# Layer norm's reciprocal root on ScalarE and VectorE, weight padding on GpSimd, and other writers in the tail of an attention and FFN kernel

## The chip, the cores and the metric

The kernel runs on one core of a Trainium2 chip. The metric is device time in microseconds (us) of one execution; the lower it is, the better. The engines are called by their names or by the short forms of the profile: TensorE (PE; PEld is its weight load), VectorE (DVE), ScalarE (ACT), GpSimd (POOL) and SyncE (SP), which issues the DMAs.

## What is computed

The input x (2048 tokens of 512) is normalised, and attention and a gated feed-forward network (FFN) both read the normalised x. There are 32 heads of 16 columns; the FFN is 1792 wide. All tensors are bfloat16.

```python
xn  = (x - mean(x)) / sqrt(var(x) + 1e-5)
q, k, v = split(xn @ wqkv)                 # 32 heads of 16
p   = softmax(q @ k.T / 4)                 # 2048 x 2048 per head
att = (p @ v) @ wo
ffn = (silu(xn @ w1) * (xn @ w3)) @ w2
out = x + att + ffn
```

## The kernel before

**The work.** Tokens stand in 16 tiles of 128. Queries are taken in four chunks of 512, heads in 8 groups of four, because a head's 16 columns, padded to 32, fill one of TensorE's four row groups. A chunk and a head group make 32 jobs; these are cut into 73 units of 128 or 256 queries (the first job in 128, 128, 256, the last four in 128 each).

Each unit goes through two phases. In phase 1 (`p1`) the scores of 128 queries and 512 keys are computed for two heads (L1041) and VectorE takes the row maximum over both at once (L1081, 128x1024 out of PSUM). 1021 such steps make up phase 1; in three of the units one row of heads takes another way, in which ScalarE helps with a `Relu` (`SPLIT`, L1150, L1070). When a unit's maxima are complete, they are negated, split in two bfloat16 numbers (`Z`, L1165, L1167, on GpSimd) and put beside the queries, by DMA transpose, or for the first two and the last four units by TensorE and a ScalarE write (`tile_QT2`, tiles called AQ, L810). Phase 2 (`p2`) can only then start for that unit: TensorE computes the transposed scores with the maximum already subtracted (L1303), and ScalarE takes the exponential of a half-tile of 128x512 (L1316), or of two in neighbouring banks at once (`exp_pair`, L1346), into slots called PT. There are 2048 half-tiles. Then `tile_PV` multiplies by V (L566); a ScalarE write to `U` (L1412), a small DMA round and GpSimd's reciprocal (L1437) and product (L1457) normalise it. The last three units skip that round: VectorE takes a reciprocal (L1402) and a product (L1404) straight from PSUM.

The FFN (`ffn_pair`) has 56 pairs of tiles, each with two ScalarE writes (L856, L860), a tanh (L850) and three GpSimd steps; the pace at which they may start is set by `FFN_LO` and `FFN_HI`, in phase 1 steps. Its results lie in 24 slots `hT`, which the output tiles free. Outputs of the first twelve token tiles are made in one PSUM tile (`tile_OUT`, L921), those of the last four in two parts: `tile_OUTA`, written by ScalarE (L938), and `tile_OUTB`, added by VectorE (L952) and stored.

**The head.** x comes in four DMAs of four tiles. Layer norm goes in eight groups of two tiles (`ln_chunk`): statistics (`STATS`: groups 0 to 3 on VectorE, L599 and L602; groups 4 to 7 on ScalarE, L589 for the mean and L593 for the squares), then in `coef` GpSimd adds epsilon (L613) and raises to the power -1/2 (L616), then in `norm` the tile is normalised (`NORM`: groups 0 to 2 on VectorE, L629; groups 3 to 7 on GpSimd, L639, for which two more small GpSimd steps first form the bias -mean times the reciprocal root, L620 and L622). TensorE transposes the tile (`tile_tr`, L664), ScalarE writes it to `xnT` (L671). Four tiles make a key block of the first head group (`tile_KT`, L695), the first tile also the first queries (`tile_QT`, L792). Their weights are padded to 32 columns by two ScalarE copies (L532, L534). Keys and queries of the other groups (`tile_heads`, L750, then a DMA through memory) and V (`tile_V`, L765) follow.

**The order of the work.** The program is not written in the order in which it runs. A planner at the end of `_build` keeps queues of items for each engine (`expq`, `miscq` and `lazyq` for ScalarE, `redq` and `dveq` for VectorE, a dictionary of queues `poolq` for GpSimd, `spq` for SyncE), each item with a cost written in the code, and at each turn emits the item that could start first (`pick_act`, `pick_dve`, `pick_pool`, `pick_sp`). For TensorE, `pick_pe` weighs the next phase 1 step, the next phase 2 scores, the next piece of an open tile (`col_cand`) and a filler matmul that keeps the array busy (`fill_cand`; into the tokens, ident against xnT). The result is a fixed order for each engine; at run time the engines only wait for each other's semaphores. Scores of phase 1 use PSUM banks 0 to 3, tiles and phase 2 share banks 4 to 7, and after the last maximum all eight. `assign` gives banks to tiles; `ROW_LEAD` and `TOL` say how much ahead of need scores are issued, `PAIR_WAIT` how long an exponential may be held for a pair, `RECENT_MIN` how many columns TensorE should have worked in the last 2.9 us of the plan.

## Time and profile before

| | us |
|---|---|
| median of 3 runs (1196.06 to 1197.04) | 1196.95 |
| the profiled execution | 1196.41 |
| its span (first to last instruction) | 1194.7 |
| VectorE busy | 1172.0 |
| ScalarE busy | 1169.5 |
| TensorE busy | 1154.4 |
| GpSimd busy | 455.3 |

The profile is of one execution. A row of the timeline gives start and duration of a run of like instructions, the engine, the line, the operation, what it writes and reads, the shapes and the count; in square brackets is the idle time of the engine before it, and what ended it. Durations overlap the next instruction of the same engine a little, so the distance from start to start is the step that counts. "Releasers" are inferred from semaphores. A group's row gives busy time, then the mean of one in ns, then the idle time in front of it. TensorE's busy time includes fillers.

### The profile page before, as it was taken

What the parts mean: (1) busy time and instruction counts of PE and PEld (TensorE: products, weight loads), DVE (VectorE), ACT (ScalarE), POOL (GpSimd) and SP (SyncE); (2) the same over time, 40 slices, a digit from 0 to 9 for tenths busy, and PEclk for the clock granted to TensorE, in tenths of its full rate; (3) what the DMA queues carried; (4) which work ended last, traced back from release to release, by engine and by line L of the source; (5) the groups of instructions that cost most, each with busy time, mean ns of one, the idle gap of its engine ahead of it and who ended that gap; (6) DMA issues with size and microseconds to landing.
All of it is one profiled execution on the core that took longest, in us unless ns stands there. A gap on an engine that the chain in (4) does not pass through costs nothing.

```text
span 1194.7 us, 33930 instructions
## 1 busy us (share of the span) xinstructions
PE 1154.4 (97%) x14172; PEld 482.5 (40%) x14172; DVE 1172.0 (98%) x1067; ACT 1169.5 (98%) x2236; POOL 455.3 (38%) x912
## 2 busy tenths in 40 slices
PE   9999999999999999999999999999999999999998
PEld 4433333333334333333334434343333333345554
DVE  8999999999999999999999999999999999999994
ACT  7899999999999999999999999999999999999997
POOL 4453752433432255343422236634222215333320
PEclk9999999999999999999999999999999999999999
DMA  6523222111111021111100122211000111000000
GB/s 183 128 59 83 68 65 79 39 33 41 38 24 36 25 71 40 41 32 31 33 20 24 35 59 51 51 31 37 22 20 20 32 33 43 19 22 18 18 18 25
DMA packets 131189, 52.17 MB, mean 44 GB/s; under 512 B 100068, under 2 KB 131036, under 8 KB 131036
## 3 DMA queue, kind: packets, MB, share of 16 engines
q1 hardware_dynamic: 131036, 50.01, 16.9%
q8 instruction: 111, 1.82, 0.7%
q14 instruction: 42, 0.34, 0.1%
HBM read 38.73 MB, written 6.74 MB: 38 GB/s over the span
## 4 chain that ended last, share of the span: by engine, by line
PE 45%; ACT 44%; DVE 6%; issue 2%; DMA 2%; POOL 1%; ACTq 0%; POOLq 0%
ACT PT L1316 30%; PE ps L562 17%; PE ps L1303 13%; PE ps L566 8%; ACT PT L1346 7%; PE ps L1041 7%; DVE part L1081 6%; ACT zg L856 2%; ACT th L850 1%; ACT ub L860 1%; DMA R<-rd 1%; ACT U L1412 1%; ACT kq L750 1%; PE ps L1663 1%; DMA Lc<-U 0%
## 5 line engine op out<-in xcount | busy, mean ns | idle before, releaser
L1081 DVE TENSOR_REDUCE part<-ps 128x2 f32<-128x1024 f32 x1018 | 1153.0, 1217 | 1.9 <-PE ps L1041 1.7
L1316 ACT ACTIVATE PT<-ps 128x512 bf16<-128x512 f32 x1680 | 889.2, 628 | 5.6 <-PE ps L1303 2.5
L1303 PE MATMUL ps<-QT,KT 32*128 32x256 bf16 (+1 forms) x4672 | 544.5, 259 | 4.7 <-ACT PT L1346 3.7
L1041 PE MATMUL ps<-KT,QT 32*128 32x512 bf16 x2042 | 424.3, 384 | 2.4 <-DVE part L1081 2.3
L1303 PEld LDWEIGHTS ps<-QT,KT 32*128 32x128 bf16 x4672 | 207.4, 92 | 214.1 <-issue 110.7
L1437 POOL TENSOR_TENSOR Rc<-Lc,mone 128x8 f32<-128x8 f32 (+1 forms) x70 | 105.9, 1513 | 294.6 <-DMA Lc<-U 294.4
L1346 ACT ACTIVATE PT<-ps 128x1024 bf16<-128x1024 f32 x184 | 194.6, 1075 | 0.0
L562 PE MATMUL ps<-xnT,ident 128*128 128x512 bf16 (+3 forms) x646 | 177.4, 341 | 17.5 <-DVE part L1081 6.7
L566 PE MATMUL ps<-PT,Vaug 128*17 128x256 bf16 (+1 forms) x4672 | 179.6, 261 | 3.1 <-ACT PT L1316 1.3
L562 PE MATMUL ps<-xnT,w 128*128 128x512 bf16 (+3 forms) x637 | 153.2, 321 | 4.7 <-ACT ub L860 1.3
L1041 PEld LDWEIGHTS ps<-KT,QT 32*128 32x128 bf16 x2042 | 107.8, 91 | 122.5 <-DVE part L1081 56.8
L566 PEld LDWEIGHTS ps<-PT,Vaug 128*17 128x17 bf16 x4672 | 84.2, 89 | 89.1 <-issue 69.5
L562 PEld LDWEIGHTS ps<-xnT,ident 128*128 128x128 bf16 x646 | 47.4, 97 | 99.9 <-ACT PT L1316 44.5
L562 PEld LDWEIGHTS ps<-xnT,w 128*128 128x128 bf16 x637 | 44.9, 97 | 85.6 <-issue 52.9
L562 PE MATMUL ps<-w,hT 128*128 128x512 bf16 (+3 forms) x330 | 75.1, 315 | 0.0
L837 POOL TENSOR_TENSOR a<-zg,ub 128x512 f32<-128x512 bf16 x56 | 64.5, 1152 | 21.6 <-ACT ub L860 21.6
L839 POOL TENSOR_TENSOR hT<-a,t 128x512 bf16<-128x512 f32 x56 | 71.0, 1267 | 2.4
L1188 POOL TENSOR_TENSOR mx<-part 128x16 f32<-128x16 f32 (+1 forms) x67 | 14.1, 210 | 141.0 <-DVE part L1081 140.5
L1457 POOL TENSOR_TENSOR wk_on<-U,R 128x256 bf16<-128x256 f32 (+1 forms) x37 | 23.3, 630 | 85.8 <-DMA R<-rd 85.6
L835 POOL TENSOR_SCALAR t<-th 128x512 f32<-128x512 bf16 x56 | 34.7, 619 | 44.8 <-ACT th L850 43.2
L1457 POOL TENSOR_TENSOR on_b<-U,R 128x256 bf16<-128x256 f32 (+1 forms) x33 | 23.4, 709 | 70.9 <-DMA R<-rd 70.9
L850 ACT ACTIVATE th<-zg 128x512 bf16<-128x512 bf16 x56 | 37.7, 673 | 0.0
(104 smaller groups left out, 574.5 us busy)
## 6 DMA issues: line engine op xcount, KB each, us to landing
w<-in_B_w_dram SPq DMA_DIRECT2D x112, 128.0 KB
R<-rd SPq DMA_DIRECT2D x55, 128.0 KB
QT<-qd SPq DMA_DIRECT2D x31, 128.0 KB
KT<-kd SPq DMA_DIRECT2D x28, 128.0 KB
PT<-in_A_x_dram SPq DMA_DIRECT2D x4, 512.0 KB
xr<-in_A_x_dram SPq DMA_DIRECT2D x16, 128.0 KB
out_dram<-osb SPq DMA_DIRECT2D x16, 128.0 KB
qd<-kq SPq DMA_DIRECT2D x15, 128.0 KB
```

The lines of the kernel that those rows point to most:

```text
L562: return e.matmul(bank(bk)[:, c0 + a:c0 + b], make_lhsT(0, 128), rhs_ap(0)[:, a:b], start=start, stop=stop, **kw)
L566: ins = e.matmul(bank(bk)[32 * i:32 * i + m, c0 + a:c0 + b], make_lhsT(i), rhs if (a, b) == (0, ncols) else rhs[:, a:b], start=start, stop ...
L837: q.append(_Item(lambda e: e.tensor_tensor(a32[:, :], zg[:, ss, :], ub[:, ss, :], ALU.mult), [("zg", ss), ("ub", ss)], [("a32",)], 1.1, 1.25))
L839: q.append(_Item(lambda e: e.tensor_tensor(hT[:, hslot(idx), :], a32[:, :], t1[:, :], ALU.mult), [("a32",), ("t1",)], [("hT", hslot(idx))] ...
L850: lazyq.append(_Item(lambda e: e.activation(th[:, ss, :], zg[:, ss, :], ACTF.Tanh), [("zg", ss)], [("th", ss)], 0.52, cb=part_done))
L1041: ins = e.matmul(bank(2 * sl + i), QT[32 * j:32 * j + 32, qs, q * 128:(q + 1) * 128], KT[32 * j:32 * j + 32, g, c_ * 512:(c_ + 1) * 512], ...
L1081: redq.append(_Item(lambda e: e.tensor_reduce(dst, pair_ap.rearrange("p (a b) -> p a b", b=512), AX.X, ALU.max), writes, [("part", par, qt ...
L1303: ins = e.matmul(bank(b)[:, i * nq:(i + 1) * nq], KT[32 * j:32 * j + 32, g, (k0 + i) * 128:(k0 + i + 1) * 128], QT[32 * j:32 * j + 32, qs, ...
L1316: expq.append(_Item(lambda e: e.activation(PT[:, sl, :], bank(b), ACTF.Exp, scale=SCALE), [("ps", b)], [("PT", sl)], _c_act(512), cb=cb, e ...
L1346: return _Item(lambda e: e.activation(PT[:, s0:s1 + 1:s1 - s0, :], ps8[:, b0:b1 + 1:b1 - b0, :], ACTF.Exp, scale=SCALE), [("ps", b0), ("ps ...
L1437: poolq["nrm"].append(_Item(lambda e: e.tensor_tensor(Rc[:, pp, 0:nl], Lc[:, pp, 0:nl], mone[:, 0:nl], ALU.pow), [("Lc", pp), ("mone",)], ...
L1457: poolq["nrm"].append(_Item(lambda e: e.tensor_tensor(onorm[ob][:, g, q0:q0 + nq], U[:, us, 0:nq], R[:, pp, 0:nq], ALU.mult), [("U", us)] ...
```

## The change

Layer norm: for groups 0 to 2 (`RSTD`), `coef` takes a square root on ScalarE, with epsilon as its bias, and a reciprocal on VectorE, in place of GpSimd's two steps. Groups 3 to 7 keep the power on GpSimd. Group 2 is now normalised by GpSimd, and GpSimd normalises like VectorE, by subtracting the mean and multiplying; the two steps that formed a bias go. A square root on a dummy stands at the very start of ScalarE's program, an exponential on a dummy behind the fourth KT write. GpSimd pads the first weights, ahead of its other layer norm items.

Order in the head: square roots come before other ScalarE writes; statistics of groups 4 to 7 (named "late") are held behind the first writes, then ranked ahead of V and q/k writes; VectorE's statistics of tiles 4 to 7 ("low") rank behind those of tiles 0 to 3; TensorE prefers transposes, KT and QT tiles; fewer other tiles may be open until the third key block is done; GpSimd may take any of four waiting normalisations.

Tail (after the last phase 1 score is issued): U, AQ and OUTA writes go to VectorE (`to_dve`); a new tile is given a bank only while fewer than two are open (`TAIL_TEN`), before five; phase 2 prefers a bank beside the one of the score before it (`TAIL_MATE`) and a pair may wait 0.05 (`TAIL_WAIT`); an OUTB tile opens once its inputs are ready, the last one step earlier. Constants of the planner change as the diff shows.

```diff
-    TOL = 0.002
-    PV_LEFT = 5
-    ROW_LEAD = 0.46
-    PAIR_WAIT = 0.02
+    TOL = -0.008
+    PV_LEFT = 4
+    ROW_LEAD = 0.44
+    PAIR_WAIT = 0.03
...
+    OUTB_EARLY = 1
+    TAIL_BUSY = 4
+    TAIL_TEN = 2
+    TAIL_MATE = 0.3
+    TAIL_WAIT = 0.05
+    TAIL_DVE = 1
...
-    HI_LEAD = 0.0
-    LAZY_MAX = 3.0
+    LOW_LAG = 0.35
+    RS_LEAD = 0.4
+    STAT_RATE = 1
+    HEAD_LAG = 0.7
+    LATE_RANK = 1.5
+    HEAD_TEN = 1
+    HEAD_KT = 2
+    STAT_LAG = 0.0
+    LAZY_MAX = 1.0
...
-    FFN_HI = 800
+    FFN_HI = 600
...
-    RECENT_MIN = 9800.0
+    RECENT_MIN = 9400.0
...
-    SPLIT_STEP = 6
+    SPLIT_STEP = 8
...
-        lnb = sb("lnb", [128, NT], FP32)
...
+        eps_t = sb("eps_t", [128, 2], FP32)
...
+        P.op("dve", lambda e: e.memset(eps_t[:, :], EPS), writes=[("eps",)], occ=0.1)
+        P.op("act", lambda e: e.activation(eps_t[:, 1:2], eps_t[:, 0:1], ACTF.Sqrt), reads=[("eps",)], writes=[("eps1",)],
+             occ=0.1)
...
-        NORM = "dddppppp"
+        NORM = "ddpppppp"
...
+        RSTD = "aaappppp"
...
-        miscq.append(_Item(lambda e: e.activation(dk, sk, ACTF.Identity), [("wk",)], [("wk0",)], 0.3,
-                           cb=lambda op: done.add("wk0")))
-        miscq.append(_Item(lambda e: e.activation(dq, sq, ACTF.Identity), [("wq",)], [("wq0",)], 0.3,
-                           cb=lambda op: done.add("wq0")))
+        poolq["ln"].append(_Item(lambda e: e.tensor_scalar(dk, sk, 1.0, 0.0, ALU.mult, ALU.add), [("wk",)], [("wk0",)], 0.4,
+                                 cb=lambda op: done.add("wk0")))
+        poolq["ln"].append(_Item(lambda e: e.tensor_scalar(dq, sq, 1.0, 0.0, ALU.mult, ALU.add), [("wq",)], [("wq0",)], 0.4,
+                                 cb=lambda op: done.add("wq0")))
...
-                        [("PT", t)], [("a32",), ("mv", t)], 0.57, 0.7))
+                        [("PT", t)], [("a32",), ("mv", t)], 0.57, 0.7, name="late" if gi > 1 else ""))
...
-                        [("PT", t), ("mv", t)], [("a32",), ("mv", t)], 0.66, 0.8, cb=lambda op: mv_done(op)))
+                        [("PT", t), ("mv", t)], [("a32",), ("mv", t)], 0.66, 0.8, cb=lambda op: mv_done(op),
+                        name="late" if gi > 1 else ""))
...
-                                      [("PT", t)], [("st", t)], 0.6, 0.7, cb=lambda op, t=t: done.add(("st", t))))
+                                      [("PT", t)], [("st", t)], 0.6, 0.7, cb=lambda op, t=t: done.add(("st", t)),
+                                      name="low" if t >= XG else "",
+                                      pred=lambda t=t: t < 8 or p1_n[0] >= 1 + (t - 8) * STAT_RATE))
...
-                                      name="hi" if t == t1 - 1 else ""))
+                                      name="low" if t >= XG else ""))
...
+                if RSTD[gi] == "a":
+                    miscq.append(_Item(lambda e: e.activation(lnt[:, sl_], mv[:, sl_, 1], ACTF.Sqrt,
+                                                              scale=1.0 / D if on_act else 1.0, bias=eps_t[:, 0:1]),
+                                       MVK + [("eps",)], [("lnt", gi)], 0.2, 0.3, name="rs" if gi < 2 else "rs2",
+                                       cb=lambda op: dveq.insert(0, _Item(
+                                           lambda e: e.reciprocal(lnr[:, sl_], lnt[:, sl_]), [("lnt", gi)],
+                                           [("lnr", gi)], 0.08, 0.2, cb=norm))))
+                    return
...
-                               0.5 + 0.16 * (t1 - t0), cb=norm if NORM[gi] == "d" else None))
-                if NORM[gi] != "d":
-                    q.append(_Item(lambda e: e.tensor_tensor(lnt[:, sl_], mv[:, sl_, 0], lnr[:, sl_], ALU.mult),
-                                   [("lnr", gi)] + MVK, [("lnt", gi)], 0.25, 0.35))
-                    q.append(_Item(lambda e: e.tensor_scalar(lnb[:, sl_], lnt[:, sl_], -1.0, 0.0, ALU.mult, ALU.add),
-                                   [("lnt", gi)], [("lnb", gi)], 0.25, 0.35, cb=norm))
+                               0.5 + 0.16 * (t1 - t0), cb=norm))
...
-                    elif NORM[gi] == "a":
-                        miscq.append(_Item(lambda e, t=t, xs=xs: e.activation(
-                            xn_sb[:, xs, :], x_sb[:, t, :], ACTF.Identity, scale=lnr[:, t:t + 1], bias=lnb[:, t:t + 1]),
-                            [("PT", t), ("lnr", gi), ("lnb", gi)], [("osb", xs)], 0.71, 0.85,
-                            cb=lambda op, t=t: tr_ready(t), pred=lambda t=t: t < 4 or ("tr", t - 4) in done))
...
-                            xn_sb[:, xs, :], x_sb[:, t, :], lnr[:, t:t + 1], lnb[:, t:t + 1], ALU.mult, ALU.add),
-                            [("PT", t), ("lnr", gi), ("lnb", gi)], [("osb", xs)], 0.7, 0.8,
+                            xn_sb[:, xs, :], x_sb[:, t, :], mv[:, t, 0:1], lnr[:, t:t + 1], ALU.subtract, ALU.mult),
+                            [("PT", t), ("lnr", gi), ("mv", t)], [("osb", xs)], 0.7, 0.8,
...
-                              [("ps", bk)], qh_keys(0, q0, nq), _c_act(nq), cb=cb)]
+                              [("ps", bk)], qh_keys(0, q0, nq), _c_act(nq), cb=cb,
+                              name="first" if name == "QTa" else "")]
...
+                if to_dve():
+                    return [_Item(lambda e: e.tensor_scalar(QT[:, qs, q0:q0 + nq], bank(bk)[:, 0:nq], 1.0, 0.0,
+                                                            ALU.mult, ALU.add),
+                                  [("ps", bk)], qh_keys(qs, q0, nq), _c_dve(nq), cb=lambda op: done.add(("AUG", u)),
+                                  name="dve")]
...
+        def to_dve():
+            return TAIL_DVE and p1_n[0] >= NP1
...
+                if to_dve():
+                    return [_Item(lambda e: e.tensor_scalar(opart[ts], bank(bk), 1.0, 0.0, ALU.mult, ALU.add),
+                                  [("ps", bk)], OP_KEYS[ts], _c_dve(512), cb=cb, name="dve")]
...
-            return _Tile("OUTB%d" % tg, groups, evac, pred=lambda: ("OUTA", tg) in done and ("ST", tg - 4) in done)
+            return _Tile("OUTB%d" % tg, groups, evac, pred=lambda: ("OUTA", tg) in done and ("ST", tg - 4) in done
+                         and all(("ON", qc, g, ts) in done for g in range(NGA, NG if tg < NT - OUTB_EARLY else NG - 1)))
...
-                    r -= MATE
+                    r -= MATE if red_n[0] < NP1 else TAIL_MATE
...
-            if b is None or len(p2_busy) >= 4:
+            if b is None or len(p2_busy) >= (4 if red_n[0] < NP1 else TAIL_BUSY):
...
+                if to_dve():
+                    return [_Item(lambda e: e.tensor_scalar(U[:, us, 0:nq], bank(bk)[:, 0:nq], 1.0, 0.0,
+                                                            ALU.mult, ALU.add),
+                                  [("ps", bk)], [("U", us)], _c_dve(nq), cb=cb, name="dve")]
...
-            if not head_tiles and sum(b in bank_tenant for b in pool_banks()) < (1 if red_n[0] < NP1 else 5):
+            if not head_tiles and sum(b in bank_tenant for b in pool_banks()) < (1 if red_n[0] < NP1 else TAIL_TEN):
...
-                    if bk not in bank_tenant and p2_n[0] == 0:
+                    if (bk not in bank_tenant and p2_n[0] == 0
+                            and sum(b_ in bank_tenant for b_ in (6, 5, 4)) < (HEAD_TEN if ("KT", 0, HEAD_KT) not in done else 3)):
...
-            return 0 if t.name.startswith("AQ") else 1.5 if t.name.startswith("V") else 2 if t.name.startswith("OUTB") else 1
+            return 0 if t.name.startswith("AQ") else 0.5 if t.name.startswith(("tr", "KT0", "QT")) else 1.5 if t.name.startswith("V") else 2 if t.name.startswith("OUTB") else 1
...
-                    if t.name.startswith("OUTB") or (t.name.startswith("PV") and int(t.name[2:]) in FAST_PV):
+                    if items[0].name == "dve" or t.name.startswith("OUTB") or (t.name.startswith("PV") and int(t.name[2:]) in FAST_PV):
...
-                if a2 <= a + PAIR_WAIT and (red_n[0] >= NP1 or sum(b_ in bank_tenant for b_ in pool_banks()) <= PAIR_TEN):
+                if a2 <= a + (PAIR_WAIT if red_n[0] < NP1 else TAIL_WAIT) and (red_n[0] >= NP1 or sum(b_ in bank_tenant for b_ in pool_banks()) <= PAIR_TEN):
...
-                    r = {"first": 0, "second": 1}.get(it.name, 2)
-                    if m is None or s < m[0] - 1e-6 or (s < m[0] + 1e-6 and r < m[2]):
-                        m = (s, k, r)
+                    r = {"rs": 0, "rs2": 0.5, "first": 0, "second": 1, "late": LATE_RANK}.get(it.name, 2)
+                    s_ = s + {"rs": -RS_LEAD, "late": STAT_LAG if ("KT", 0, 0) in done else HEAD_LAG}.get(it.name, 0.0)
+                    if m is None or s_ < m[3] - 1e-6 or (s_ < m[3] + 1e-6 and r < m[2]):
+                        m = (s, k, r, s_)
...
-                        if it.name == "hi":
-                            s = max(s - HI_LEAD, 0.0)
-                        if b is None or s < b[0] - 1e-6:
-                            b = (s, q, k)
+                        r = s + (LOW_LAG if it.name == "low" and p1_n[0] == 0 else 0.0)
+                        if b is None or r < b[3] - 1e-6:
+                            b = (s, q, k, r)
...
-                if q and okp(q[0]):
-                    s = cand("pool", q[0])
-                    if b is None or s < b[0] - 1e-6:
-                        b = (s, q)
-            return None if b is None else (b[0], lambda: emit_item("pool", b[1], 0))
+                for i, it in enumerate(q[:4 if k == "nx" else 1]):
+                    if okp(it):
+                        s = cand("pool", it)
+                        if b is None or s < b[0] - 1e-6:
+                            b = (s, q, i)
+            return None if b is None else (b[0], lambda: emit_item("pool", b[1], b[2]))
...
+        act_stats.append(_Item(lambda e: e.activation(eps_t[:, 1:2], eps_t[:, 0:1], ACTF.Exp), [("eps",)], [("eps1",)], 1.4,
+                               pred=lambda: ("KT", 0, NQC - 1) in done))
```

## The prediction

> **What bounds the kernel now.** I read the engine totals first, then busy time by stretch, the costliest groups, and the order of time at the head and the tail. The totals (busy microseconds, share of the span, instructions):
>
> ```profile
> PE 1154.4 (97%) x14172; PEld 482.5 (40%) x14172; DVE 1172.0 (98%) x1067; ACT 1169.5 (98%) x2236; POOL 455.3 (38%) x912
> ```
>
> Three engines are full, so shares alone decide nothing. Busy time by stretch (length, then PE, PE weight loads, DVE, ACT, POOL, granted clock, DMA share, GB/s):
>
> ```profile
> 0.00:9.37 9.37, 7.09 (x47) 5.50 (x48) 5.79 (x16) 1.87 (x3) 3.40 (x16) 1.00 0.83 253
> 9.37:33.10 23.73, 23.49 (x177) 10.57 (x175) 22.29 (x29) 23.63 (x59) 12.30 (x28) 1.00 0.54 146
> 33.10:45.96 12.86, 12.86 (x84) 4.80 (x84) 12.58 (x12) 7.22 (x14) 5.05 (x9) 1.00 0.20 59
> 45.96:1170.50 1124.54, 1092.34 (x13318) 450.36 (x13316) 1124.33 (x1001) 1119.26 (x2129) 433.13 (x859) 1.00 0.16 40
> 1170.50:1189.20 18.70, 17.63 (x529) 10.74 (x519) 5.10 (x11) 17.53 (x34) 1.46 (x2) 1.00 0.10 29
> 1189.20:1194.70 5.50, 1.02 (x33) 0.54 (x33) 1.94 (x3) 0.01 (x1) 0.00 (x0) 0.71 0.07 24
> ```
>
> VectorE's order of time gives the start of its row maxima (24 of them in 27.30 us, 1.13 each without a break):
>
> ```profile
> 13.60 27.30 DVE L1081 TENSOR_REDUCE part<-ps 128x2 f32<-128x1024 f32 x24 [1.44 <-PE ps L1041]
> ```
>
> From there VectorE is full to 1170.5, where its last maximum ends and the stretches are cut. ScalarE goes on to 1189.2 and has the tail to itself. Its costliest groups, with mean ns of one:
>
> ```profile
> L1316 ACT ACTIVATE PT<-ps 128x512 bf16<-128x512 f32 x1680 | 889.2, 628 | 5.6 <-PE ps L1303 2.5
> L1346 ACT ACTIVATE PT<-ps 128x1024 bf16<-128x1024 f32 x184 | 194.6, 1075 | 0.0
> ```
>
> They are 1680 + 2 x 184 = 2048 exponential half-tiles. ScalarE after VectorE's last maximum:
>
> ```profile
> 1169.57 0.61 ACT L938 ACTIVATE zg<-ps 128x512 f32<-128x512 f32 x1
> 1170.05 0.62 ACT L1316 ACTIVATE PT<-ps 128x512 bf16<-128x512 f32 x1
> 1170.61 0.28 ACT L1412 ACTIVATE U<-ps 128x128 f32<-128x128 f32 x1
> ...
> 1172.38 0.28 ACT L810 ACTIVATE QT<-ps 128x128 bf16<-128x128 f32 x1
> ...
> 1180.26 1.02 ACT L1346 ACTIVATE PT<-ps 128x1024 bf16<-128x1024 f32 x1
> 1181.16 8.05 ACT L1316 ACTIVATE PT<-ps 128x512 bf16<-128x512 f32 x16
> ```
>
> The last unit's own queries are ready at 1172.38 + 0.28 = 1172.66, and its 16 half-tiles take about 8. ScalarE needs until 1189.2, so it is some 8 us behind what VectorE would allow. Of these rows a single steps by (8.05 - 0.13)/16 = 0.495 (0.13 is the overlap of one, 0.62, with the next), the pair by 1181.16 - 1180.26 = 0.90: a pair saves 0.09.
>
> So the end is ScalarE's: its work plus its idle time up to 1189.2 (by the stretches 7.50 before 9.37, 0.10 to 33.10, 5.64 to 45.96, 5.28 to 1170.5, 1.17 after), then 5.5 us of a last P times V, a reciprocal, a product and a store. I therefore count changes in ScalarE's work and idle time; VectorE counts only where it would fall 8 us back.
>
> **The change, part by part.**
>
> *Square root and reciprocal.* VectorE and GpSimd in the head:
>
> ```profile
> 6.68 0.16 DVE L602 BATCH_NORM_AGGREGATE mv<-stats 128x2 f32<-128x6 f32 x1
> ...
> 8.08 0.70 DVE L629 TENSOR_SCALAR osb<-PT,mv,lnr 128x512 bf16<-128x512 bf16 x2
> ```
> ```profile
> 18.11 0.19 POOL L620 TENSOR_TENSOR lnt<-mv,lnr 128x2 f32<-128x2 f32 x1
> 18.39 0.19 POOL L622 TENSOR_SCALAR lnb<-lnt 128x2 f32<-128x2 f32 x1
> 18.69 1.52 POOL L639 TENSOR_SCALAR osb<-PT,lnr,lnb 128x512 bf16<-128x512 bf16 x2
> ```
>
> From the aggregate's end (6.84) to the normalisation (8.08) pass 1.24 us, over two GpSimd steps. The trace has no square root and no such reciprocal. The square root, of 128x2, lies between nothing and the 0.28 of the 128x128 QT row; the reciprocal between the 0.16 of the aggregate and the 0.70 of two normalisations. I take 0.2 and, the operands being as small as the aggregate's, 0.17; with three hand-overs of 0.1 that is 0.7 us. It saves 0.5 for tiles 0 and 1, and 0.9 for tiles 2 and 3, since the small operations of tiles 4 to 7 now come last; at 0.70 for the reciprocal, nothing. VectorE drops two normalisations (0.70) and takes three reciprocals (0.5). GpSimd takes those two normalisations (1.52), off the path to the first maximum. For tiles 6 to 15 it drops L620 and L622: 18.69 - 18.11 = 0.58 us less in each pair's chain.
>
> *Padded weights and order.* On ScalarE:
>
> ```profile
> 0.78 1.28 ACT L476 ACT_TABLE_LOAD   x1 [0.78 <-PEq L1927]
> ...
> 7.84 0.42 ACT L532 ACTIVATE wk_on<-wk_on 128x256 bf16<-128x256 bf16 x1 [5.17 <-DMA wk_on<-in_A_wqkv_dram]
> 9.37 1.08 ACT L671 ACTIVATE xnT<-ps 128x512 bf16<-128x512 bf16 x2 [1.11 <-PE ps L664]
> 10.34 0.42 ACT L534 ACTIVATE wk_on<-wq 128x256 bf16<-128x256 bf16 x1
> 10.68 1.08 ACT L671 ACTIVATE xnT<-ps 128x512 bf16<-128x512 bf16 x2
> 11.66 0.62 ACT L589 ACTIVATE a<-PT 128x512 f32<-128x512 bf16 x1
> ```
>
> L534 costs 10.68 - 10.34 = 0.34 of ScalarE's path; L532 lay in idle time. On GpSimd both stand at the front of a queue taken in order and wait for wq's load; behind them stands first the coefficient of tiles 6 and 7, whose statistics VectorE now takes last. The statistic at 11.66, ahead of the first KT write, now ranks behind it. The first KT write, and the first maximum with it, comes about 1.1 us earlier (0.5 to 0.9, and part of 0.34 and 0.62; bounds 0 and 1.9): 12.5 for 13.60. For VectorE that is slack upon slack. For ScalarE it is 0.5 less idle time before its first transpose write, and the 0.34. The first square roots and the extra one at the start fall in its idle 7.50; the third adds 0.2. SP's queue gets nothing new.
>
> *Statistics of tiles 8 to 15 ahead of the V and q/k writes.* ScalarE between 9.37 and 32.8, grouped, and then in order of time:
>
> ```profile
> L765 ACT ACTIVATE Vaug<-ps 128x512 bf16<-128x512 f32 x4 | 2.5, 618 | 0.0
> ...
> L750 ACT ACTIVATE kq<-ps 128x512 bf16<-128x512 f32 x3 | 1.8, 598 | 0.0
> ```
> ```profile
> 32.53 0.20 ACT L593 ACTIVATION_READ_ACCUMULATOR a<-PT,mv 128x1 f32 x1
> ...
> 39.89 0.69 ACT L695 ACTIVATE KT<-ps,kbias 128x512 bf16<-128x512 f32 x1 [1.61 <-PE ps L562]
> ...
> 45.96 1.02 ACT L1346 ACTIVATE PT<-ps 128x1024 bf16<-128x1024 f32 x1
> ```
>
> Seven such writes stood among the statistics, 7 x 0.48 = 3.4 us (0.48 is the step of the like write at 1169.57). Ranked behind, they leave the statistics done near 29 instead of 32.73, and with 0.58 less on GpSimd, and TensorE serving transposes first, the fourth KT write ends 4 to 5 us before 40.58. The exponentials, 5.4 us behind it, start near 41.5. The writes are not gone: they come in the 12 us between, paced by TensorE, which is full there, at about one per maximum (1.13 us). ScalarE then has some 5 of writes, 2.5 of transposes and KT and 1.4 of table load in those 12 us: 3.4 idle, for 5.64. Gain 2.2; bounds 0 and 5.6.
>
> *The second table.* The first ScalarE instruction is now a square root, and a dummy exponential stands behind the fourth KT write; queued behind it are V writes and the first unit's queries. By the row at 0.78 one more load is 1.28, with the dummy +1.4, charged in full as work. The Trainium skill, "ScalarE: Activation LUTs", section "What ACT_TABLE_LOAD costs", puts each switch of set at 1283 ns and a drain of 1380 ns; the first agrees with the row, the second no run here shows. With the drain the forecast would be an estimated 1193.7.
>
> *The tail.* Once the last scores for a maximum are issued, U, QT and OUTA writes go to VectorE, which idled there. Three ScalarE steps go: 0.48 (1169.57 to 1170.05) and about 0.15 each for the QT and U rows (0.28 less the overlap): 0.8, or 0.3 if OUTA falls ahead of the switch. VectorE pays one 512-column write (no row; its 1024-column maximum of 1.13 bounds it), ahead of nothing but the last maximum's finish. Fewer tile tenants (2 for 5) and a bias for neighbouring banks pair more scores: of some 29 single half-tiles up to 24, 12 x 0.09 = 1.1; I take 0.9, bounds 0 and 1.3. The last OUTB still waits for the same product, so the 5.5 us stay.
>
> *The planner's constants.* SPLIT_STEP 8 for 6 leaves three split rows: units 40, 46, 52 before (58 has no second query tile), 40, 48, 56 after. FFN_HI 600 brings the FFN's ScalarE work forward, its sum unchanged; its tiles 24, 38 and 52 wait for hidden slots that earlier outputs free, so ScalarE's lag grows in the middle and is back by the end. PAIR_WAIT 0.03 for 0.02 lets more scores pair; ROW_LEAD and TOL shift their issue by 0.01 to 0.02. No row shows what the plan makes of it: between 10% fewer (+1.7) and 30% more (-5.0) of the 184 pairs, and ScalarE's idle 5.28 anywhere from 3 to 8. I take -1.5 (17 pairs), nearer to no change, as the one bound that is relaxed works one way.
>
> **Sum** on ScalarE's end: idle -0.5 and -2.2, work -0.3 + 0.2 + 1.4 - 0.8 - 0.9 - 1.5, together -4.6. The profiled execution took 1196.41 (span 1194.7 and 1.71 around it), so 1191.8; the median of the runs, 1196.95, is 0.54 above it: 1192.3.
>
> **Rivals.**
>
> *A: the head is hidden anyway.* ScalarE's idle 5.64 stays because TensorE, busy 12.86 of 12.86 there, paces the tiles it waits for, and the load's 1.4 comes on top: -0.5 - 0.3 + 0.2 + 1.4, and half of the tail's 1.7 and of the pairs' 1.5, is -0.8: 1196.1. For it: that stretch. Against it: its KT writes waited for normalised tokens first, and exponentials need only KT.
>
> *B: slower, by TensorE's clock.* RECENT_MIN 9400 for 9800 asks 4% fewer columns of each 2.9 us, and a TOL 0.010 lower leaves fillers out. The granted clock is 1.00 in each stretch up to 1189.2, and 0.71 in the last, where TensorE is busy 1.02 of 5.5 us: idleness does lower it. The fillers (ident against xnT):
>
> ```profile
> L562 PE MATMUL ps<-xnT,ident 128*128 128x512 bf16 (+3 forms) x646 | 177.4, 341 | 17.5 <-DVE part L1081 6.7
> ```
>
> Without them TensorE works 977 of 1194.7, 82%, so at half clock a stretch takes 1.64 times its length. It decides, slower by 2.4, from (4.6 + 2.4)/0.64 = 11 us at half clock, a mean clock of 0.995; 20 us give 12.8 - 4.6 = +8.2: 1205. Against: TensorE idles 40 us in all, in pieces. The Trainium skill, "TensorE: Matmul & The Clock Gate", Part 1, lets the clock drop after an idle window of about 3.4 us; by that rule no stretch before 1189 qualifies, and the trace agrees.
>
> *C: more.* 30% more pairs (3.5 above my 1.5) and the idle 3.4 filled too: -11.5, but VectorE, 1.1 earlier, allows 8 + 1.1: 1188.
>
> **How the numbers follow.** Forecast 0.62, A 0.17, B 0.09, C 0.12. 0.2%, or 2.4 us, is about what a measurement of this kernel can tell from no change: faster is under 1194.6, which is the forecast, C and a sixth of A, 0.77; same 0.14; slower 0.09. The forecast's own range is 1189.5 to 1194.5. Reaching into C and A without B, the range is 1187 to 1196.3.
>
> **What would show it.** First maximum near 12.5; fourth KT write ending near 36; a table load of 1.28 behind it; first exponential near 41.5; ScalarE idle about 3.4 us between; no U, QT or OUTA write on ScalarE after the last maximum and 11 or more pairs there; last maximum near 1169.4, last exponential near 1184.6. It is wrong if VectorE idles over 8 us in the body, if pairs drop under 150, if the clock leaves 1.00, or if square and copy need further table loads in the head.

## The result, and the profile after

The changed kernel takes 1209.7 us (median of 6 runs, 1206.72 to 1210.87) beside 1197.0 for the kernel before on the same chip: a ratio of 1.0099, interval [1.0084, 1.0113]. It is slower by 1%, where 0.4% faster was forecast. The profiled execution took 1210.87 us, its span 1209.1.

Totals, the clock by slice and the group of VectorE's maxima from the page of the changed kernel (busy time, mean ns of one, then the idle time in front of the group and its releaser), and then the same group of the kernel before:

```profile
PE 1128.6 (93%) x13964; PEld 472.6 (39%) x14121; DVE 1173.5 (97%) x1070; ACT 1172.5 (97%) x2222; POOL 468.5 (39%) x899
...
PEclk8899999999999999999999999999999999999999
...
L1112 DVE TENSOR_REDUCE part<-ps 128x2 f32<-128x1024 f32 x1018 | 1154.3, 1217 | 16.4 <-PE ps L1072 16.2
```
```profile
L1081 DVE TENSOR_REDUCE part<-ps 128x2 f32<-128x1024 f32 x1018 | 1153.0, 1217 | 1.9 <-PE ps L1041 1.7
```

VectorE and ScalarE are busy for as long as before, to a few us. But VectorE now stands still for 16.4 us in front of its maxima, for 1.9 before, waiting for scores, and the clock is below full in the first two slices, so in the first 60 us. ScalarE's order of time shows that the whole loss is there:

```profile
53.43 0.69 ACT L713 ACTIVATE KT<-ps,kbias 128x512 bf16<-128x512 f32 x1 [0.69 <-PE ps L579]
54.14 1.28 ACT L1891 ACT_TABLE_LOAD   x1
55.43 0.20 ACT L1891 ACTIVATE eps_t<-eps_t 128x1 f32<-128x1 f32 x1
...
59.96 1.09 ACT L1347 ACTIVATE PT<-ps 128x512 bf16<-128x512 f32 x2
...
1202.27 1.17 ACT L1347 ACTIVATE PT<-ps 128x512 bf16<-128x512 f32 x2
```

The first exponential starts at 59.96 where it was 45.96, 14.0 later; the last ends at 1203.44 where it was 1189.2, 14.2 later. What holds the head up stands in GpSimd's groups. First the normalisation of the kernel before, then that of the changed one:

```profile
L639 POOL TENSOR_SCALAR osb<-PT,lnr,lnb 128x512 bf16<-128x512 bf16 x10 | 7.6, 769 | 0.5
```
```profile
L657 POOL TENSOR_SCALAR osb<-PT,mv,lnr 128x512 bf16<-128x512 bf16 x12 | 24.8, 2075 | 0.5
```

It is the same instruction on the same shape, with subtract and multiply in place of multiply and add. One takes 2.07 us for 0.77, and GpSimd has 24.8 us of them in the first 51. Between its pairs it also waits three times, 7.7 us in all, for ScalarE's statistics, which come late because ScalarE in turn waits for TensorE's transposes (11.1 us between 8 and 56). TensorE's waits in the changed kernel, up to 70 us (total, times, longest), and then its head in stretches of 2 us (columns as in the prediction's stretches):

```profile
PE ps L682 <- POOL osb L657: 6.8, 6, 2.4
```
```profile
16.00:18.00 2.00, 0.91 (x6) 0.34 (x4) 1.18 (x1) 0.00 (x0) 2.00 (x2) 0.77 0.76 176
18.00:20.00 2.00, 1.09 (x8) 0.51 (x7) 1.23 (x1) 0.60 (x1) 2.00 (x2) 0.50 0.41 115
...
24.00:26.00 2.00, 1.98 (x9) 0.55 (x7) 1.20 (x1) 0.49 (x2) 2.00 (x2) 0.50 0.00 0
...
28.00:30.00 2.00, 1.95 (x12) 0.60 (x10) 1.98 (x2) 2.00 (x6) 0.39 (x2) 1.00 0.00 0
...
36.00:38.00 2.00, 2.00 (x7) 0.53 (x6) 1.23 (x1) 0.94 (x4) 0.97 (x3) 0.50 0.00 0
```

TensorE waits for the transposes' input six times; GpSimd is full (2.00 of 2.00) in the first of these rows. The clock falls to 0.50 twice, at about 17 and 34 us. It comes back only at about 27 and 44, although TensorE is busy again long before (1.98, 2.00). In these two spells TensorE does its work at half the clock, and VectorE gets one maximum in most of the 2 us, in which it did nearly two before.

### The profile page after: what moved, and what is told of

The parts are those of the page before. It is cut to its first block, busy times and chain, and to the rows that moved or that the text cites. A ratio compares the mean times of both kernels' runs of the same rounds, so it can differ in the third digit from the quotient of the medians.

```text
span 1209.1 us, 33674 instructions
## 1 busy us (share of the span) xinstructions
PE 1128.6 (93%) x13964; PEld 472.6 (39%) x14121; DVE 1173.5 (97%) x1070; ACT 1172.5 (97%) x2222; POOL 468.5 (39%) x899
## 4 chain that ended last, share of the span: by engine, by line
ACT 58%; PE 31%; DVE 7%; issue 2%; POOL 2%; DMA 1%; another core or an unknown queue 0%; ACTq 0%; POOLq 0%
ACT PT L1347 42%; PE ps L579 12%; ACT PT L1377 10%; PE ps L1334 8%; DVE part L1112 6%; PE ps L583 5%; PE ps L1072 5%; ACT zg L880 1%; ACT U L1447 1%; ACT th L874 1%; POOL osb L657 1%; ACT ub L884 1%; ACT kq L768 1%; DVE stats L617 0%; DMA PT<-in_A_x_dram 0%
## 5 line engine op out<-in xcount | busy, mean ns | idle before, releaser
L1112 DVE TENSOR_REDUCE part<-ps 128x2 f32<-128x1024 f32 x1018 | 1154.3, 1217 | 16.4 <-PE ps L1072 16.2
L1347 ACT ACTIVATE PT<-ps 128x512 bf16<-128x512 f32 x1646 | 871.8, 623 | 4.8 <-PE ps L1334 3.1
L1334 PE MATMUL ps<-QT,KT 32*128 32x256 bf16 (+1 forms) x4672 | 529.5, 259 | 15.2 <-ACT PT L1377 9.8
L1072 PE MATMUL ps<-KT,QT 32*128 32x512 bf16 x2042 | 418.1, 385 | 5.1 <-DVE part L1112 2.0
L1334 PEld LDWEIGHTS ps<-QT,KT 32*128 32x128 bf16 x4672 | 199.8, 92 | 215.4 <-issue 107.1
L1377 ACT ACTIVATE PT<-ps 128x1024 bf16<-128x1024 f32 x201 | 211.6, 1074 | 0.3 <-PE ps L1334 0.3
L579 PE MATMUL ps<-xnT,ident 128*128 128x512 bf16 (+3 forms) x624 | 174.4, 339 | 24.9 <-ACT PT L1377 8.3
L1072 PEld LDWEIGHTS ps<-KT,QT 32*128 32x128 bf16 x2042 | 103.8, 91 | 135.1 <-DVE part L1112 67.3
L579 PE MATMUL ps<-xnT,w 128*128 128x512 bf16 (+3 forms) x558 | 138.6, 325 | 9.9 <-ACT U L1447 2.2
L579 PEld LDWEIGHTS ps<-xnT,ident 128*128 128x128 bf16 x688 | 50.6, 97 | 108.0 <-ACT PT L1347 51.7
L579 PE MATMUL ps<-w,hT 128*128 128x512 bf16 (+3 forms) x298 | 69.5, 318 | 2.8 <-ACT U L1447 1.6
```

Of the source, the lines that this page charges most:

```text
L579: return e.matmul(bank(bk)[:, c0 + a:c0 + b], make_lhsT(0, 128), rhs_ap(0)[:, a:b], start=start, stop=stop, **kw)
L1072: ins = e.matmul(bank(2 * sl + i), QT[32 * j:32 * j + 32, qs, q * 128:(q + 1) * 128], KT[32 * j:32 * j + 32, g, c_ * 512:(c_ + 1) * 512], ...
L1112: redq.append(_Item(lambda e: e.tensor_reduce(dst, pair_ap.rearrange("p (a b) -> p a b", b=512), AX.X, ALU.max), writes, [("part", par, qt ...
L1334: ins = e.matmul(bank(b)[:, i * nq:(i + 1) * nq], KT[32 * j:32 * j + 32, g, (k0 + i) * 128:(k0 + i + 1) * 128], QT[32 * j:32 * j + 32, qs, ...
L1347: expq.append(_Item(lambda e: e.activation(PT[:, sl, :], bank(b), ACTF.Exp, scale=SCALE), [("ps", b)], [("PT", sl)], _c_act(512), cb=cb, e ...
L1377: return _Item(lambda e: e.activation(PT[:, s0:s1 + 1:s1 - s0, :], ps8[:, b0:b1 + 1:b1 - b0, :], ACTF.Exp, scale=SCALE), [("ps", b0), ("ps ...
```

## The experiments

Two theories stood at the start. T1: the subtracting operation on GpSimd is slow, and the rest follows from it. T2: the new order and queues of the head make the loss, whatever the operation. Times are medians, ratios are to runs of the kernel before on the same chip.

### The operation

*The changed kernel with multiply and add again,* for groups 2 to 7, with the two small bias steps.

```diff
-   tensor_scalar(xn, x, mv, lnr, subtract, mult)
+   tensor_scalar(xn, x, lnr, lnb, mult, add)     # lnb = -mean * lnr, two steps before
```

> The changed kernel, but GpSimd normalises as before by multiply and add, with the two small steps that form the bias (also for tiles 4 and 5). Theory 1, the operation: one normalisation takes 0.77 us again instead of 2.07, VectorE's idle time before its maxima falls from 16.4 us to under 3, the first exponential comes near 42 to 46 instead of 59.96, the clock stays 1.00, and the time is 1188 to 1196. Theory 2, the order: the new ranks and the smaller number of open tiles in the head leave TensorE without work and its clock drops, and the slow operation only lies beside it: VectorE still idles over 8 us and the time stays over 1202.

Measured 1198.64, ratio 1.0020 [1.0011, 1.0029]. One normalisation took 768 ns, VectorE stood still for 2.7 us in front of its maxima, the first exponential came at 45.28 and the clock stayed at full, all as T1 had it. By the ratios 0.79 of the 0.99% went, some 9.5 of 12 us. The operation is the main cause. But the time is above T1's 1188 to 1196: it is still not faster than before.

*The kernel before with the slow operation alone,* without the bias steps. The planner's cost of 0.7 us for it stays, as in the changed kernel.

```diff
-   tensor_scalar(xn, x, lnr, lnb, mult, add)
+   tensor_scalar(xn, x, mv, lnr, subtract, mult)
```

> The kernel before with one part of the change alone: GpSimd normalises (tiles 6 to 15) by subtracting the mean and multiplying, without the two steps for the bias. Theory 1, the operation: ten normalisations at 2.07 us; five pairs of 0.9 + 4.1 us in a row on GpSimd cannot end before about 39 to 42 instead of 35.97, the fourth KT write comes 3 to 7 us later, and the time is 1199 to 1206. Theory 2, the order: within 2 us of before.

Measured 1206.86, ratio 1.0083 [1.0069, 1.0097]. In its groups:

```profile
L634 POOL TENSOR_SCALAR osb<-PT,mv,lnr 128x512 bf16<-128x512 bf16 x10 | 20.7, 2076 | 0.5
```

This one edit, which even saves instructions, makes most of the loss by itself. Here the clock is the lesser part of it: one of the five runs, at a mean clock of 0.999, still took 1204.37, and the other four, at 0.993 to 0.996, took 1206.32 to 1207.73.

*Which form is slow?* Multiply then subtract, and, in a second kernel, add (of the negated mean) then multiply, both in the changed kernel.

> The changed kernel, but GpSimd normalises by multiplying with the reciprocal root and subtracting mean times root (multiply first, subtract second; one small step more than the change, one less than before). If it is subtracting that is slow on GpSimd, one takes about 2.07 us and the time stays near 1209. If it is the order (multiply first is fast), one takes 0.77 and the time is 1188 to 1196.

> The changed kernel, but GpSimd normalises by adding the negated mean and multiplying by the reciprocal root (one small step for the negation, instead of two). If subtracting alone is what is slow, one normalisation takes 0.77 us and the time is within 2.5 us of the first experiment's 1198.6. If adding first and multiplying second is slow too, it takes about 2.07 and the time is over 1205.

Measured 1208.59 (1.0105 [1.0092, 1.0119]) and 1198.6 (1.0018 [1.0005, 1.0030]). The group of the first, then of the second:

```profile
L666 POOL TENSOR_SCALAR osb<-PT,lnr,lnb 128x512 bf16<-128x512 bf16 x12 | 24.8, 2074 | 0.5
```
```profile
L666 POOL TENSOR_SCALAR osb<-PT,lnb,lnr 128x512 bf16<-128x512 bf16 x12 | 9.1, 767 | 0.5
```

Neither the order of the two operations nor the operand from `mv` matters, only that one of them subtracts.

*The planner is told the true cost* (2.06 for 0.7), the operation stays slow.

```diff
-   [("osb", xs)], 0.7, 0.8,
+   [("osb", xs)], 2.06, 2.16,
```

> The changed kernel with nothing changed but the planner's cost for a GpSimd normalisation, 2.06 instead of 0.7 us. Theory 1, the operation: GpSimd still paces the head, but TensorE gets fillers and other tiles in the gaps; the clock stays 1.00, VectorE still idles 5 to 12 us and the time is 1199 to 1207. If the clock that fell, rather than GpSimd's pace, cost most of the 16 us: VectorE idles under 5 us and the time is under 1198.

Measured 1201.52, ratio 1.0043 [1.0030, 1.0057]. Its stretches of the head, and then those of the changed kernel:

```profile
13.00:34.00 21.00, 18.92 (x118) 7.60 (x119) 15.38 (x14) 19.28 (x48) 20.27 (x17) 1.00 0.36 83
34.00:60.00 26.00, 26.00 (x247) 11.61 (x243) 25.08 (x25) 19.47 (x38) 16.72 (x20) 1.00 0.53 138
```
```profile
13.00:34.00 21.00, 15.72 (x76) 5.29 (x77) 13.78 (x12) 13.81 (x33) 17.93 (x13) 0.76 0.29 67
34.00:60.00 26.00, 23.51 (x129) 8.82 (x133) 19.03 (x19) 15.07 (x31) 13.43 (x13) 0.80 0.30 90
```

GpSimd is as slow as ever, but the plan puts other work into TensorE's gaps (18.92 of 21.00 for 15.72), the clock stays at 1.00, and VectorE stands still for 6.6 us instead of 16.4. By the ratios, of the 0.99% some 0.56 came from an order planned with a wrong cost, 0.23 from the slow operation under a right plan (1.0043 to 1.0020), and 0.20 is left with the fast one. Each of these parts is known to about 0.15 to 0.2. How much of the 0.56 is the fallen clock, and how much the waits themselves, was not separated.

### The other parts

*The fast operation with the constants of before;* then *the fast operation with the tail of before;* then *the kernel before with the new tail alone.*

> The first experiment's kernel (GpSimd multiplies and adds) with the planner's constants of before (TOL, PV_LEFT, ROW_LEAD, PAIR_WAIT, LAZY_MAX, FFN_HI, RECENT_MIN, SPLIT_STEP). It had 1198.6 where 1188 to 1196 was expected. If the new constants cost what the head and tail bring, the time falls to 1193 to 1196. If the constants are neutral, it stays within 2 us of 1198.6.

> The first experiment's kernel with the tail of before (no write moved to VectorE, five open tiles, no bias for pairs, OUTB tiles as before). If the tail brings the 1.7 us of the prediction's sum, this is slower: 1199.5 to 1201.5, with 3 to 5 pairs after the last maximum instead of 12. If the tail brings nothing, the time is 1198.6 or less.

> The kernel before with the new tail alone. By the prediction's sum 1.7 us faster than before, 1194 to 1195.5, last maximum to last exponential 17 us or less instead of 18.7. If the tail brings nothing, within 1 us of before, or slower.

Measured 1199.2 (1.0018 [1.0009, 1.0028]), 1200.34 (1.0029 [1.0020, 1.0039]) and 1194.66 (0.9983 [0.9974, 0.9991]). The constants do nothing that can be seen. The tail is worth 2.0 us on the kernel before, and there it gives the one version that is faster than both kernels. On the changed head it is worth 1.7 by the medians, which are from two chips, and 1.1 by the ratios, whose intervals overlap. VectorE and ScalarE at its end:

```profile
1170.85 0.17 DVE L1235 TENSOR_REDUCE negm<-part 128x4 f32<-128x16 f32 x1
1171.35 0.68 DVE L953 TENSOR_SCALAR zg<-ps 128x512 f32<-128x512 f32 x1
1171.95 0.28 DVE L1431 TENSOR_SCALAR U<-ps 128x128 f32<-128x128 f32 x1
1172.15 0.28 DVE L817 TENSOR_SCALAR QT<-ps 128x128 bf16<-128x128 f32 x1
```
```profile
1187.06 0.62 ACT L1334 ACTIVATE PT<-ps 128x512 bf16<-128x512 f32 x1
```

From VectorE's last maximum to the end of the last exponential pass 16.8 us, before 18.7. The 1199.2 of the first and the 1194.66 of the third differ by the changed head alone, with its operation mended: it costs 4.5 us, where the forecast's terms for it add up to a gain of 1.4.

### Why the head does not gain

Three parts were undone one at a time in the 1199.2 version. H1 puts its loss on tiles 4 and 5, now normalised by GpSimd; H2 on the second table and the square roots, which are work for ScalarE; H3 on the new order.

> The head is still some 4.5 us dearer with the fast operation (1199.2 with the old constants, against 1194.7 for the tail alone). Here tiles 4 and 5 are normalised by VectorE again, all else as in the kernel with the fast operation and the old constants. H1 (these two on GpSimd stand behind others and keep the second key block late): VectorE's wait of 1.62 us at about 22 us shrinks below 0.5, the first exponential comes 1 to 2 us earlier, and the time falls by 2 to 4 us, to 1195 to 1197. H2 (the second table and the square root are what costs) and H3 (the order of the head): within 1 us of 1199.2, as VectorE only exchanges 0.7 us of work for 1.5 us of GpSimd's.

> All eight groups take the power on GpSimd again; the square roots, the reciprocals, the dummies at both ends and so the second table load are gone, all else as in the kernel with the fast operation and the old constants. H2 (second table, 1.28 us, with the square roots 0.9 us on ScalarE, while ScalarE sets the end): 1.5 to 3 us less, 1196 to 1197.7, though the first maximum comes 0.5 to 1 us later. H1 and H3: within 1 us of 1199.2, or up to 2 us more, since GpSimd has 1 us more to do for each of three pairs of tiles.

> The head's order is that of the kernel before: ScalarE's statistics of tiles 8 to 15 are not held back, VectorE's of tiles 4 to 7 not ranked late, transposes and keys get no preference, three tiles may be open, and GpSimd takes its normalisations in order; the square roots, padding, normalisers and old constants stay. H3 (the order pushes V and query writes behind the first exponentials and so loads the body): more V and query writes stand ahead of the first exponential (15 to 16 instead of 14) and the time falls by 2 to 4 us, to 1195 to 1197. H1 and H2: within 1 us of 1199.2, or slower if the order had been worth what it was made for.

Measured 1198.4 (1.0015 [1.0006, 1.0023]), 1210.95 (1.0114 [1.0098, 1.0129]) and 1200.57 (1.0036 [1.0023, 1.0049]). H1 is worth under 1 us: the wait at 22 us went, but VectorE then waited 2.17 us at 64. The order is no loss, so H3 fails; whether it gains the 1.4 cannot be said, as the intervals overlap. The middle one was no clean test. (Its edit, and that of its repetition below, also holds TensorE's fillers back until the first four tiles are transposed.) GpSimd, then VectorE in it:

```profile
9.33 0.41 POOL L550 TENSOR_SCALAR wk_on<-wq 128x256 bf16<-128x256 bf16 x1 [1.08 <-DMA wq<-in_A_wqkv_dram]
9.82 0.19 POOL L640 TENSOR_SCALAR lnt<-mv 128x2 f32<-128x2 f32 x1
```
```profile
17.45 28.38 DVE L1121 TENSOR_REDUCE part<-ps 128x2 f32<-128x1024 f32 x25 [4.82 <-PE ps L1081]
...
72.91 2.36 DVE L1121 TENSOR_REDUCE part<-ps 128x2 f32<-128x1024 f32 x2 [5.18 <-PE ps L1081]
```

The first power stood behind the two paddings, which wait for the weights' load, and the first maximum came 5 us late: GpSimd can pad first only because ScalarE has taken the powers. The second wait, of 5.18 us, has another cause, which the stall described below explains. So the test was repeated with the paddings in GpSimd's last queue, and beside it the square roots alone were put on the best version.

```diff
-   poolq["ln"].append(pad wk); poolq["ln"].append(pad wq)
+   poolq["pad"].append(pad wk); poolq["pad"].append(pad wq)
```

> As the version with all powers on GpSimd (1210.95), but the two paddings stand in GpSimd's last queue, so that the powers no longer wait behind them for the load of the weights. If that place was what put the first maximum off to 17.45 us and cost the 11.7 us: GpSimd's first power step starts near 7.1 instead of 9.8, the first maximum near 13.5 to 14.5, and the time is below 1201. H2 then expects 1196 to 1197.7 (1199.2 less the second table and the square roots), H3 1198.5 to 1200.5. If the place did not matter: above 1206.

> The kernel before with the new tail, and of the head's changes only the square roots and reciprocals for tiles 0 to 5 with the two dummies; normalisers, padding by ScalarE and order stay. The version without it took 1194.66. H2 (second table, square roots and the padding's place make the rest of the loss): ScalarE's work grows by 1.3 + 0.9 + 0.2, the first maximum comes 0.3 to 0.7 us earlier, and the time is 1196 to 1197.5. H3 (the new order and VectorE's later end lose it): 1193.5 to 1195.5.

Without second table and square roots: 1198.37 (1.0023 [1.0008, 1.0038]), 0.8 less, and too wide to set H2 apart from H3. The square roots alone: 1204.61 (1.0063 [1.0048, 1.0077]), 10 us more than without them, which no theory had. Yet its head came earlier, as the prediction had said; ScalarE:

```profile
36.50 0.69 ACT L714 ACTIVATE KT<-ps,kbias 128x512 bf16<-128x512 f32 x1 [1.12 <-PE ps L573]
37.20 1.28 ACT L1890 ACT_TABLE_LOAD   x1
...
43.41 1.02 ACT L1377 ACTIVATE PT<-ps 128x1024 bf16<-128x1024 f32 x1
```

The fourth KT write and the first exponential are 3.7 and 2.9 us earlier than in the version without the square roots (40.24 and 46.31). The loss is later, at 62 us. SyncE's DMA issues and its wait in front of the last of them, the row of TensorE's waits between 58 and 82 us, stretches of this version, and SyncE's issues in the version without the square roots:

```profile
46.12 0.46 SPq L563 DMA_DIRECT2D w<-in_B_w_dram  x1
...
52.73 1.30 SPq L1242 DMA_TRANSPOSE Zs<-Z  x1
62.23 1.17 SPq L1238 DMA_DIRECT2D QT<-Zs  x2
```
```profile
SPq L1238 <- DMA Zs<-Z: 8.1, 1, 8.1
```
```profile
PE ps L1334 <- DMA QT<-Zs: 2.4, 1, 2.4
```
```profile
64.00:66.00 2.00, 1.21 (x7) 0.50 (x9) 0.00 (x0) 0.17 (x1) 0.00 (x0) 0.56 0.25 67
...
74.00:76.00 2.00, 2.00 (x25) 0.48 (x19) 1.23 (x1) 1.25 (x3) 0.21 (x1) 0.50 0.10 15
```
```profile
45.04 0.43 SPq L558 DMA_DIRECT2D w<-in_B_w_dram  x1
...
53.76 1.29 SPq L1229 DMA_TRANSPOSE Zs<-Z  x1
...
58.48 1.15 SPq L1225 DMA_DIRECT2D QT<-Zs  x2
```

The third unit's maxima are transposed by a DMA at 52.73, behind a load of 1792 KB of FFN weights (L563). The next step waits until 62.23 for it; in the version without the square roots it was issued 4.7 us after the transpose, not 9.5. There the same load stands ahead of the transpose too, but 8.7 us ahead instead of 6.6, so that more of it is over: the DMA engines' mean busy share falls to 0.35 by 56 to 58 us, and is still 1.17 with the square roots. TensorE runs dry for 2.43 us, once, and its clock is then at half until 78, while VectorE loses 8 us. H4: the bulk load starts that. So it was put behind the third unit's round, and as a control the same was done without the square roots.

```diff
-   later_dma(w2 <- w2_v)
+   later_dma(w2 <- w2_v, pred=("AUG", 2) in done and p1_n[0] >= 48)
```

> As the version with the square roots alone (1204.61), but the load of 1792 KB of FFN weights, issued there at 46.12 us ahead of the third unit's transposed maxima, is issued behind that unit's round and the next keys, near 65 us. H4 (the bulk load holds up the small transfer of the maxima, TensorE runs dry at 62 us for 2.4 us and its clock is halved until 78, which costs VectorE 8 us): the transfer takes under 5 us instead of 9.5, VectorE's idle time between 60 and 80 falls below 1.5 us, the clock stays at 1.00 and the time is 1193 to 1197. If the bulk load has nothing to do with it: 1203 to 1206.

> The control: the kernel before with the new tail (1194.66), with the same later bulk load and nothing of the head's change. There the third unit's maxima were not late (4.7 us from issue to issue of the next step), so by H4 the time stays within 1 us of 1194.7; it rises if the later load collides with something else.

Measured 1197.77 (1.0011 [1.0001, 1.0020]) and 1205.4 (1.0062 [1.0040, 1.0084]). SyncE and a stretch in the first:

```profile
53.06 1.29 SPq L1242 DMA_TRANSPOSE Zs<-Z  x1
57.00 1.16 SPq L1238 DMA_DIRECT2D QT<-Zs  x2
```
```profile
60.00:68.00 8.00, 7.95 (x201) 4.32 (x201) 8.00 (x8) 8.00 (x19) 1.02 (x1) 1.00 0.25 76
```

The transfer takes 3.9 us, VectorE is full, the clock is 1.00, and 6.8 of the 10 us are gone: H4 holds, though the time is 0.8 us above its range. The same stall is in the version with all powers on GpSimd (1210.95): there the transpose is issued at 56.55, 5.6 us behind the load, and the next step 9.5 us later, and the clock is at 0.50 between 70 and 80 us. That accounts for its second wait.

The control missed: it stayed 10.7 us above 1194.66, because the later load now holds up another small transfer, which leaves a dry spell at another place. SyncE, GpSimd, ScalarE and TensorE in the control, and a stretch behind it:

```profile
68.79 0.48 SPq L558 DMA_DIRECT2D w<-in_B_w_dram  x1
69.38 1.16 SPq L1455 DMA_DIRECT2D Lc<-U  x1
```
```profile
77.30 1.03 POOL L1459 TENSOR_TENSOR Rc<-Lc,mone 128x4 f32<-128x4 f32 x1 [4.68 <-DMA Lc<-U]
```
```profile
79.72 0.60 ACT L867 ACTIVATE zg<-ps 128x512 bf16<-128x512 f32 x1 [2.86 <-POOL a L848]
```
```profile
80.37 0.60 PE L1321 MATMUL ps<-QT,KT 32*128 32x256 bf16 x2 [2.37 <-ACT zg L867]
```
```profile
90.00:96.00 6.00, 6.00 (x56) 1.78 (x59) 3.76 (x4) 3.50 (x7) 3.41 (x8) 0.50 0.17 38
```

The small load of a unit's sums (`Lc`), issued right behind the bulk load, reaches GpSimd at 77.30, 7.9 us later. GpSimd's FFN product (L848) stands behind the reciprocal that waits for it, ScalarE behind that product, and TensorE behind ScalarE. The control's six runs are spread: two took 1199.43 and 1199.62 at a mean clock of 0.997, four 1205.26 to 1207.46 at 0.987 to 0.991.

What remains between 1197.77 and 1194.66 is 3.1 us. It is not a clean price of the square roots, as the two versions also differ in the load's place, which costs 4.8 us even in the control's quickest run; but the 1197.77 version shows no such stall. Totals of the version without square roots, then with them and the later load:

```profile
PE 1125.4 (94%) x14015; PEld 480.5 (40%) x14172; DVE 1172.7 (98%) x1070; ACT 1168.2 (98%) x2226; POOL 456.8 (38%) x912
```
```profile
PE 1132.3 (95%) x14065; PEld 479.0 (40%) x14213; DVE 1174.0 (98%) x1074; ACT 1171.9 (98%) x2221; POOL 452.8 (38%) x906
```

ScalarE's work is 3.7 us more. Of that, 1.28 is the table, 0.2 the dummy behind it and 3 x 0.29 the square roots, 2.35 together; the rest was not taken apart. The first exponential is 2.5 us earlier (43.76), and the last ends 2.3 later (1190.02 for 1187.68). Up to the first exponential ScalarE has 10.0 us of idle time for 13.6, so 3.6 were saved there; behind it 8.2 for 5.9, so 2.2 came back. Together with the work that is the 2.3: ScalarE sets the end, and the earlier start did not pay for the added work. That H2 makes most of the 3.1 fits these numbers but is not shown, and what makes the 4.5 of the whole head stays open.

## Why the prediction was wrong, step by step

**The step that failed: "GpSimd takes those two normalisations (1.52), off the path to the first maximum", and the 0.58 "less in each pair's chain".** Both take GpSimd's instruction at the 1.52 for two of the row of multiply and add. With a subtraction it takes 2.07 for one. For a pair of tiles that adds 2.6 us to a chain that was to lose 0.58, and the six pairs in turn hold up TensorE's transposes and ScalarE's statistics. The diff had the operation in plain sight; the prediction should have treated it as one that the trace did not show, between 0.77 and no upper bound, as it did the square root.

**What became of the sum.** ScalarE's end is its work plus its idle time up to there: 1169.5 + 19.7 = 1189.2 before. The forecast took 1.9 from the work and 2.7 from the idle time. In the changed kernel the end is 1203.44, with 3.0 more work and 11.2 more idle time; with the fast operation it is 1191.02, with 2.9 more work and 1.1 less idle time. So the operation made some 12 us of idle time, and the work was wrong by 4.8 whatever the operation. For that reason rival A (1196.1) does not fit the 1198.64 either.

**Rival B named a part of the mechanism, at another place and price.** TensorE's clock did fall, but through gaps in the head, not through the fillers' constants, and the slow operation costs time without it too. 0.56% of the 0.99% came with the mis-told plan, in which the clock fell to 0.50; with the plan told the cost it was 1.00 throughout the head.

**The head's moves came where the operation was fast, and did not pay.** First maximum "12.5": 12.45 in the changed kernel. "Fourth KT write ends 4 to 5 us before 40.58", first exponential "near 41.5": with the fast operation 39.5 and 45.28, for the second key block was late, and VectorE waited 1.62 us for it until 23. With the square roots alone they were 37.2 and 43.41, so 3.4 and 2.6 us earlier than before. Up to the first exponential ScalarE's idle time, 13.2 before, was 12.1 with the fast operation, where the forecast had it 2.7 lower.

**ScalarE's added work was sized low.** The table and dummy came to 1.48 (1.4 forecast), a square root to 0.29 (0.2), a reciprocal to 0.15 (0.17); only one of three square roots was charged, as the first ones were to fall into idle time. The Trainium skill, "ScalarE: Activation LUTs", section "What ACT_TABLE_LOAD costs", adds a drain of 1380 ns to each switch. The trace disagrees: the load starts at 54.14, 0.02 us after the KT write in front of it ends, and the next ACTIVATE starts at 55.43, right at the load's end.

**The tail was right, in part by luck:** -1.7 forecast, -2.0 measured on the kernel before. No U, QT or OUTA write is left on ScalarE after the last maximum, as forecast. Of pairs there are 9 for 3 there (12 in the changed kernel), which at 0.09 each is 0.5 for the 0.9; and 0.6 came from idle time (0.58 for 1.17) that the forecast did not count.

**The constants were wrong by the whole of their 1.5:** there are more pairs (201 in the changed kernel, 188 with the fast operation, 184 before), but with the fast operation 1.0020 (new constants) and 1.0018 (old) is no difference.

## What to carry to other kernels

An instruction with another arithmetic operation is another instruction: on GpSimd write a subtraction as an addition of the negated value, and give the planner the time of the very form that it issues. A kernel whose engines are all full has no cheap gap: one dry spell of TensorE of 2.4 us cost 8 us here, so look for the late transfer behind a bulk load before believing a saving of one or two. A control can fall into the same stall at another place, so follow its waits as well. Work moved to the engine that sets the end must be counted in full, and time won at the start only as far as that engine is seen to start and stay busy earlier.

## What the runs showed that was not expected

GpSimd's two-operation instruction on 128x512 bfloat16 takes 767 to 769 ns with multiply and add in either order, and 2074 to 2076 ns when one of the two subtracts. The Trainium skill, "GPSIMD Engine Reference", section 3.1, gives 769 ns for 512 elements as the best case of GpSimd's loop; the fast form agrees with it, and it says nothing of the subtraction.

TensorE's clock fell to half after single waits of 2.43 us and 2.37 us, and stayed there for some 14 and 27 us, although TensorE was busy for nearly all of that time (6.00 of 6.00 from 70 to 76 us in the first, 12.00 of 12.00 from 84 to 96 in the second). In the kernel before, whose clock stays at 1.00 up to 1189 us, no wait of TensorE behind its first instruction is longer than 1.4 us. The Trainium skill, "TensorE: Matmul & The Clock Gate", Part 1, has the clock drop after an idle window of about 3.4 us and return after as long a busy one. Here less idle time was enough, and the return took longer. At half clock the waits went on in small pieces, which may have kept it down; that was not tested.
